# A new table of unit order and of engines for flexible units, in a cluster-attention and maxout-FFN kernel on one core

## The chip, the core and the metric

The kernel runs on one core of one Trainium2 chip. The metric is the device time in microseconds (us) of one execution. A measurement of this kernel can tell a difference of about 0.2% (1.4 us) from none.

## What is computed

Four batches of eight heads; each head has 768 queries and 768 keys of 64 numbers. A query sees only the keys whose nearest centroid (of 16 per head) is the query's own. The attention's output goes through a feed-forward network (FFN) with three first matrices, of whose products the largest is kept.

```python
q_assign = argmax(q_n . c_n);  k_assign = argmax(k_n . c_n)      # 16 clusters per head
mask     = q_assign[:, None] == k_assign[None, :]
scores   = where(mask, scale * q @ k.T, -1e9)
attn     = softmax(scores);  x = attn @ v                        # (4, 8, 768, 64) -> (3072, 512)
h        = max(x @ w1, x @ w2, x @ w3)                           # 512 -> 768
out      = h @ w_out                                             # 768 -> 512
```

The result is wanted nearly as exact as fp32, so most operands of a matmul are held as a high and a low f16 half, and a product is made of three matmuls.

## The kernel before

The program writes its work as 3077 **units**, each a closure that issues one instruction or one matmul group on one engine: TensorE (PE), VectorE (DVE), ScalarE (ACT), GpSimd (POOL), or a DMA on SyncE's queue (SP). No scheduler moves them at run time: each engine runs its instructions in the order in which they were written, and waits at an instruction whose inputs are not there or whose buffer is still in use.

- **prep** (lines 690 to 885), once for each of 4 batches and 4 pairs of heads: q and k are loaded, a power of two that scales them is found (L733 on DVE or L731 on ACT, then small instructions L739 to L762), both are cut into halves (L810/L812, L378/L382, L818), and the cluster of each row becomes 32 further rows of the operands (L577 to L648), so that the score matmul itself adds the mask.
- **v_prep** does the same for v. **weights** loads the four matrices in 24 pieces (`piece`, L1019 to L1030: a cast L1024 or L1026 on ACT or POOL, then one DVE instruction L1030), finds scales (L1070, for w_out L1094 to L1108) and cuts into halves (L1041/L1043, L987/L989, L1046).
- **visit**: 32 visits (batch, half of the queries, pair of heads), each of six tiles of 128 queries by 768 keys. A tile (`tile_units`) is a score product on PE into PSUM (L1256 and L1258, buffer `big`, of which there are three), the row minimum on DVE (L1267), the exponential on ACT (L1273), for later batches the row scale (L1293, L1294, L1321/L1323), and the two halves `hl` (L378, L380 or L382; L1279 or L1332). They are then transposed by a DMA (L1282); of the first 40 steps every second is transposed on PE instead (L1304) and split from PSUM (L378 or L382, then L1312). After six tiles comes the product with v on PE (`av`, L1207, 36 matmuls), and its result is split into `x16` (L380/L382 and L1179).
- **ffn**: eight groups of 384 tokens. A group has 18 first products (`hid`, L1413, 12 matmuls into the PSUM buffer `one`, of which there are two); each is evicted (`ev`: L380 on ACT or L382 on DVE for the first of three, L1427 on DVE for the others, which takes the maximum), each third eviction is cut into halves (L987/L989, L1142); then three output products (`outp`, L1468, 18 matmuls), evicted by L380 or L382 and stored.

The order around everything is a table: `ORDER` lists the 3077 unit numbers. `HANDS` gives a letter (V, S, G, Q for DVE, ACT, POOL, SP) for each of those units that may run on more than one engine. Two of the few lines that use them:

```python
u.hand = engines[next(hands)] if u.pick else None     # Plan.run: the engine of a flexible unit
u.fn(u.hand) if u.pick else u.fn()                    # Plan.run: issued in ORDER's order
```

A unit that needs a buffer takes the place that came free first, so the table also sets which place of `big`, `one` or `stage` is used by whom.

Of the kernel before, what the change touches and what calls it, by code (L numbers as in the profile page):

```python
# [1534 lines left out]
```

## Time and profile before

| what | us |
|---|---|
| median of three runs | 711.62 (711.52 to 713.02) |
| span of the profiled execution, first to last instruction | 709.1 |
| what lies around it (median less span) | 2.5 |
| PE busy in the span | 665.5 |
| DVE busy | 599.0 |
| ACT busy | 483.6 |
| POOL busy | 403.3 |

A row of the windows names a stretch and says how long each engine was busy in it. A row of the instruction groups gives line, engine, operation, what is written and read, the count, the summed busy time, the mean of one in ns, and the idle time of the engine just before, with what ended it. In a timeline row the first number is the start, the second the duration.

### The profile page before, as it was taken

What the parts mean: (1) busy time and instruction counts of PE and PEld (TensorE: products, weight loads), DVE (VectorE), ACT (ScalarE), POOL (GpSimd) and SP (SyncE); (2) the same over time, 40 slices, a digit from 0 to 9 for tenths busy, and PEclk for the clock granted to TensorE, in tenths of its full rate; (3) what the DMA queues carried; (4) which work ended last, traced back from release to release, by engine and by line L of the source; (5) the groups of instructions that cost most, each with busy time, mean ns of one, the idle gap of its engine ahead of it and who ended that gap; (6) DMA issues with size and microseconds to landing.
All of it is one profiled execution on the core that took longest, in us unless ns stands there. A gap on an engine that the chain in (4) does not pass through costs nothing. (4 is left out here: it accounts for less than half of the span.)

```text
span 709.1 us, 13176 instructions
## 1 busy us (share of the span) xinstructions
PE 665.5 (94%) x4505; PEld 389.9 (55%) x4505; DVE 599.0 (84%) x1470; ACT 483.6 (68%) x841; POOL 403.3 (57%) x374
## 2 busy tenths in 40 slices
PE   3778778998999999999999999999999999999997
PEld 1554545555456655565555555655555646564663
DVE  7998999999998878999989888999899967784231
ACT  6988989989865657787767647786667775651000
POOL 3677887888656564857566545666584551531000
PEclk8578999999999999999999999999999999999999
DMA  6698878779798879998979998999999785775001
GB/s 225 199 216 182 207 210 205 188 174 202 168 196 188 172 126 217 197 185 195 215 156 194 179 189 181 185 196 196 197 194 178 145 164 112 148 158 125 1 1 60
DMA packets 297795, 121.03 MB, mean 171 GB/s; under 512 B 273024, under 2 KB 284160, under 8 KB 297728
## 3 DMA queue, kind: packets, MB, share of 16 engines
q1 hardware_dynamic: 297728, 120.20, 80.0%
q8 instruction: 35, 0.57, 0.3%
q14 instruction: 32, 0.26, 0.1%
HBM read 31.49 MB, written 6.29 MB: 53 GB/s over the span
## 5 line engine op out<-in xcount | busy, mean ns | idle before, releaser
L1267 DVE TENSOR_SCALAR_CACHE_REDUCE big<-big,nsc 128x768 f32<-128x768 f32 x192 | 192.7, 1016 | 11.4 <-PE big L1258 10.8
L1413 PE MATMUL one<-x,w16a 128*128 128x384 f16 x1152 | 197.0, 326 | 0.2
L1279 POOL TENSOR_TENSOR hl<-e,hl 128x768 f16<-128x768 f32 x86 | 144.4, 1682 | 61.1 <-ACT hl L378 34.2
L1413 PEld LDWEIGHTS <-w16a 128*128 128x128 f16 x1152 | 111.5, 98 | 75.7 <-issue 2.9
L1273 ACT ACTIVATE e<-big,nm 128x768 f32<-128x768 f32 x116 | 104.4, 901 | 49.7 <-DVE big L1267 32.3
L1256 PE MATMUL big<-qk 128*128 128x512 f16 (+1 forms) x384 | 96.6, 334 | 12.2 <-ACT e L1273 9.4
L1207 PE MATMUL big<-pt,v 128*64 128x384 f16 x1152 | 101.8, 330 | 2.4 <-ACT e L1273 1.4
L1413 PE MATMUL one<-x,w16b 128*128 128x384 f16 x576 | 98.9, 326 | 1.0 <-DVE worow L1098 1.0
L1258 PE MATMUL big<-qk 96*128 96x512 f16 (+1 forms) x384 | 96.1, 331 | 0.1
L1273 ACT ACTIVATE big<-big,nm 128x768 f32<-128x768 f32 x76 | 66.3, 872 | 43.7 <-DVE big L1267 35.3
L1207 PEld LDWEIGHTS <-v 128*64 128x64 f16 x1152 | 70.0, 111 | 33.2 <-issue 9.8
L1413 PEld LDWEIGHTS <-w16b 128*128 128x128 f16 x576 | 55.7, 98 | 40.1 <-issue 3.4
L1332 DVE SCALAR_TENSOR_TENSOR hl<-big,rs,hl 128x768 f16<-128x768 f32 x72 | 72.7, 1011 | 4.6 <-ACT hl L380 3.6
L380 ACT ACTIVATE hl<-big,rs 128x768 f16<-128x768 f32 x62 | 55.7, 898 | 27.3 <-issue 10.7
L1323 POOL TENSOR_SCALAR e<-e,rs 128x768 f32<-128x768 f32 x37 | 34.0, 919 | 65.9 <-DVE rs L1294 47.1
L1256 PEld LDWEIGHTS <-qk 128*128 128x128 f16 x384 | 35.3, 99 | 43.7 <-issue 22.1
L378 ACT CAST hl<-e 128x768 f16<-128x768 f32 x60 | 49.8, 831 | 5.3 <-POOL e L1323 4.5
L1258 PEld LDWEIGHTS <-qk 96*128 96x128 f16 x384 | 38.2, 100 | 27.1 <-issue 2.6
L818 POOL TENSOR_TENSOR qk<-stage,qk 128x768 f16<-128x768 f32 x26 | 43.8, 1686 | 9.2 <-ACT qk L378 5.5
L1468 PE MATMUL one<-wo,vf_h 128*128 128x512 f16 x216 | 48.3, 379 | 0.5 <-ACT o L380 0.4
L1468 PE MATMUL one<-wo,wf_h 128*128 128x512 f16 x216 | 48.3, 379 | 0.0
L1427 DVE SCALAR_TENSOR_TENSOR wf_h<-one,wf_h 128x384 f32<-128x384 f32 x48 | 26.5, 553 | 20.2 <-PE one L1413 19.6
(203 smaller groups left out, 1002.0 us busy)
## 6 DMA issues: line engine op xcount, KB each, us to landing
stage<-in_qk_dram SPq DMA_DIRECT2D x32, 384.0 KB, 4.3
wd<-in_moe_w_dram SPq DMA_DIRECT2D x18, 512.0 KB, 4.2
out_dram<-o SPq DMA_DIRECT2D x24, 256.0 KB, 2.9
qk<-qk SPq DMA_DIRECT2D x15, 384.0 KB, 4.3
qk<-qk SPq DMA_DIRECT2D x30, 192.0 KB, 3.5
stage<-in_v_dram SPq DMA_DIRECT2D x12, 384.0 KB, 4.0
wd<-in_moe_w_out_dram SPq DMA_DIRECT2D x6, 512.0 KB, 3.8
qk<-cl_t SPq DMA_DIRECT2D x60, 48.0 KB, 2.3
```

Of the source, the lines that this page charges most:

```text
L378: eng.copy(out, x)
L380: eng.activation(out, x, AF.Copy, scale=k)
L818: eng.tensor_tensor(t()[:, AQ, i], x(), t()[:, BQ, i], op=ALU.subtract)
L1207: nc.tensor.matmul(t()[D * i : D * i + D, 0:nb], v()[:, i, kt, a], pts[i % len(pts)]()[:, rows[i], c * QT + kt, :], start=(m == 0), stop=( ...
L1256: nc.tensor.matmul(t()[:, lo:hi], aq[:, qs], ak[:, lo:hi], start=True, stop=False)
L1258: nc.tensor.matmul(t()[:, lo:hi], bq[0:K2, qs], bk[0:K2, lo:hi], start=False, stop=True)
L1267: nc.vector.tensor_scalar(s, s, -SCALE if exact else nscs[:, b, pr : pr + 1], 3.0e38, op0=ALU.mult, op1=ALU.min, accum_out=nm())
L1273: nc.scalar.activation(e(), t()[:, 0:S], AF.Exp, bias=nm(), scale=-1.0, accum_out=r)
L1279: eng.tensor_tensor(hl()[:, 1, :], e(), hl()[:, 0, :], op=ALU.subtract)
L1332: eng.scalar_tensor_tensor(hl()[:, 1, :], e(), r(), hl()[:, 0, :], op0=ALU.mult, op1=ALU.subtract)
L1413: nc.tensor.matmul(t()[:, 0:nb], w16[jt // JA][:, jt % JA, wa, i, ct], x16[b, gi, ct]()[:, xa, 0:nb], start=(m == 0), stop=(m == 3 * CT - 1),)
L1468: nc.tensor.matmul(t()[:, 0:DM], h16(jt)[:, ha, tt * P : (tt + 1) * P], wo16[0][:, jt, wa, :], start=(m == 0), stop=(m == 3 * JT - 1),)
```

## The change

`ORDER` and `HANDS` have new contents; no other line is touched. The table has five lines fewer, so a line number in the changed kernel is five smaller (L1267 becomes L1262). All units, their dependencies, the number of buffers and the sum of work on PE and on SP (475 and 372 units) stay. Units on DVE go from 1272 to 1265, on ACT from 619 to 608, on POOL from 339 to 357. The first and last lines of each table:

```diff
 ORDER = """
-1 0 18 19 51 52 173 445 151 2-5 7 6 54 53 8-15 20 21 30 22-24 39 25 26 40 27 55 28 16 31 33 36 35 56 41 57 63
+0 3 1 2 4 19 18 5-14 21 15 30 16 52 51 20 22 17 53-56 23 173 174 24 57 39 25 63 58 26 62 27 59 28 33 40 151 176
...
 HANDS = """
-VVSSSSSSVVSSSSSSGSGSGGQQGVSSGSGSVGQQGVSSSSGSSGQQGVSGGSVGSSGSSGGSGVSSGSSGSSGSSGVGSGSSGVSGSGGVVSGSGGSGGGGGVSGGSS
+VVSSSSSSVVSSVSVSGSGSGGQQGVSSGVGSGGQQGSSSSSGSSGQQGVSSGSGGSSGGSGGSSVSSGSSGSSGSSSVGSGSSGGSGSSSVSSGSGGSGGSGGVGSGSSGS
...
```

What the table moves is read from the order of the instructions on an engine. **First place: DVE, around the weight pieces of w_out, before the fifteenth first product of the first FFN group.** `wf` and `worow` belong to the pieces of w_out, `vf_h` to the FFN's evictions, `big` to the score tiles. Before:

```order
L626 STREAM_TRANSPOSE cl_t_1639<-onehot2_99 128x768
L1030 SCALAR_TENSOR_TENSOR wf_1838<-wd_1852,top_111 128x512
L1267 TENSOR_SCALAR big_1946,nm_1983<-big_1946,nsc_117 128x768
L1094 TENSOR_REDUCE worow_121<-wf_1838 128x1
L1142 TENSOR_TENSOR vf_h_1497<-vf_h_1311,vf_h_1497 128x384
L1102 TENSOR_SCALAR worow_121<-worow_121 128x1
L382 TENSOR_SCALAR vf_h_1311<-one_1951 128x384
L1098 TENSOR_SCALAR worow_121<-worow_121 128x1
```

The same place in the change:

```order
L1025 SCALAR_TENSOR_TENSOR wf_1835<-wd_1861,top_111 128x512
L1262 TENSOR_SCALAR big_1949,nm_1954<-big_1949,nsc_117 128x768
L1097 TENSOR_SCALAR worow_121<-worow_121 128x1
L1089 TENSOR_REDUCE worow_121<-wf_1835 128x1 x2
L1093 TENSOR_SCALAR worow_121<-worow_121 128x1
L1262 TENSOR_SCALAR big_1958,nm_1997<-big_1958,nsc_117 128x768
L1422 SCALAR_TENSOR_TENSOR vf_h_1320<-one_1965,vf_h_1320 128x384
L1097 TENSOR_SCALAR worow_121<-worow_121 128x1 x2
L1093 TENSOR_SCALAR worow_121<-worow_121 128x1
L621 STREAM_TRANSPOSE cl_t_1633<-onehot2_99 128x768
L1422 SCALAR_TENSOR_TENSOR vf_h_1320<-one_1979,vf_h_1320 128x384
```

The eviction L382 of the product before has left DVE, and the last conversion of a w_out piece, two row maxima and the transposition L626 stand later against the FFN's products.

**Second place: ACT, at the same point of the program.** Before:

```order
L1273 ACTIVATE e_1923,rs_1578<-big_1861,nm_1902 128x768
L987 CAST x16_1925<-xs_1826 128x384
L378 CAST hl_1927<-e_1923 128x768
L1041 ACTIVATE wf_1838<-wf_1838,w_s_1911 128x512
L987 CAST vf_h_1497<-vf_h_1311 128x384
L987 CAST wo16_1103<-wf_1838 128x512
L1273 ACTIVATE e_1991,rs_1824<-big_1946,nm_1983 128x768
```

In the change:

```order
L1036 ACTIVATE wf_1589<-wf_1589,w_s_1923 128x512
L982 CAST vf_h_1527<-vf_h_1320 128x384
L982 CAST x16_1942<-xs_1833 128x384
L1184 ACTIVATE rs_1570<-rs_1570 128x6
L375 ACTIVATE vf_h_1320<-one_1925 128x384
L1268 ACTIVATE e_1946,rs_1770<-big_1912,nm_1920 128x768
L726 ACTIVATE qk_1879,q_m2_1880<-stage_1900 128x768
```

The eviction (L375, before L382 on DVE) is now ACT's, between a row sum and an exponential.

**Third place: ACT at the start, from the first maxima of pair 1 to the first four mask rows.** Before:

```order
L731 ACTIVATE qk_170,q_m2_171<-stage_0_156 128x768
L731 ACTIVATE qk_170,q_m2_171<-stage_0_154 128x768
L488 ACTIVATE cw_100<-one_180 64x4x16 x4
L380 ACTIVATE qk_186<-stage_0_150,q_s_211 128x768
L380 ACTIVATE qk_186<-stage_0_152,q_s_211 128x768
L847 COPY qk_186<-qk_186 64x1536 x3
```

In the change:

```order
L483 ACTIVATE cw_100<-one_166 64x4x16 x4
L726 ACTIVATE qk_195,q_m2_196<-stage_0_184 128x768
L375 ACTIVATE qk_168<-stage_0_153,q_s_227 128x768
L375 ACTIVATE qk_168<-stage_0_155,q_s_227 128x768
L842 COPY qk_168<-qk_168 64x1536 x4
L373 CAST qk_195<-stage_0_186 128x768
```

One of the two maxima (L731) has gone to DVE, and the four copies stand together.

## Rows read from the trace of the kernel before

**Rows 1.** The page, first part: busy time, share of the span, instructions.

```profile
PE 665.5 (94%) x4505; PEld 389.9 (55%) x4505; DVE 599.0 (84%) x1470; ACT 483.6 (68%) x841; POOL 403.3 (57%) x374
```

**Rows 2.** Windows: stretch, its length, busy time (and count) by engine, clock, DMA.

```profile
0.00:115.70 115.70, 82.67 (x554) 53.43 (x555) 105.39 (x227) 99.30 (x177) 82.58 (x99) 0.87 0.80 204
115.70:160.28 44.58, 42.16 (x306) 25.66 (x307) 44.28 (x107) 41.10 (x76) 36.22 (x32) 1.00 0.77 194
160.28:211.90 51.62, 48.86 (x332) 27.50 (x331) 50.53 (x135) 41.73 (x71) 34.03 (x32) 1.00 0.91 189
211.90:640.00 428.10, 426.60 (x2920) 247.78 (x2919) 377.88 (x965) 294.65 (x509) 247.66 (x208) 1.00 0.90 177
640.00:709.10 69.10, 65.20 (x399) 35.55 (x397) 20.95 (x39) 6.84 (x12) 2.76 (x4) 1.00 0.18 46
```

**Rows 3.** PE's waits from 115.7 to 211.9: total us, times, longest.

```profile
PE one L1413 <- DVE worow L1098: 1.0, 1, 1.0
PE one L412 <- DVE vf_h L1427: 0.7, 1, 0.7
```

**Rows 4.** PE's timeline at the fifteenth first product of FFN group one.

```profile
160.28 2.11 PE L1413 MATMUL one<-x,w16b 128*128 128x384 f16 x12 [0.96 <-DVE worow L1098]
```

**Rows 5.** DVE's timeline just ahead of that product.

```profile
156.28 1.42 DVE L1030 SCALAR_TENSOR_TENSOR wf<-wd,top 128x512 int32<-128x512 int32 x1
...
158.55 0.68 DVE L1094 TENSOR_REDUCE worow<-wf 128x1 f32<-128x512 f32 x1
...
159.68 0.54 DVE L382 TENSOR_SCALAR vf_h<-one 128x384 f32<-128x384 f32 x1
```

**Rows 6.** Instruction groups of DVE by form, whole span.

```profile
L626 DVE STREAM_TRANSPOSE cl_t<-onehot 128x768 f16<-128x768 f16 x14 | 13.6, 972 | 0.2
...
L1279 DVE TENSOR_TENSOR hl<-e,hl 128x768 f16<-128x768 f32 x10 | 10.6, 1057 | 0.3
...
L382 DVE TENSOR_SCALAR hl<-e 128x768 f16<-128x768 f32 x13 | 7.2, 552 | 0.6 <-ACT e L1321 0.6
...
L733 DVE TENSOR_REDUCE q_m<-stage 128x1 f32<-128x768 f32 x7 | 6.5, 945 | 0.3 <-DMA stage<-in_qk_dram 0.3
...
L1043 DVE TENSOR_SCALAR wf<-wf,sc_s 128x512 f32<-128x512 f32 x2 | 1.5, 740 | 0.0
```

**Rows 7.** Instruction groups of ACT by form, whole span.

```profile
L380 ACT ACTIVATE vf_h<-one 128x384 f32<-128x384 f32 x18 | 8.7, 486 | 0.7 <-PE one L1413 0.7
L1024 ACT CAST top<-wd 128x512 f16<-128x512 bf16 x11 | 8.6, 778 | 1.1 <-DVE wf L1030 0.8 <-DMA wd<-in_moe_w_dram 0.3
```

**Rows 8.** ACT's waits from 115.7 to 160.28.

```profile
ACT e L1273 <- DVE big L1267: 2.8, 4, 1.0
```

**Rows 9.** DVE's timeline at the two waits for PE between 53 and 59 us.

```profile
53.96 1.02 DVE L1267 TENSOR_SCALAR_CACHE_REDUCE big<-big,nsc 128x768 f32<-128x768 f32 x1 [0.99 <-PE big L1258]
...
58.66 0.56 DVE L1226 TENSOR_TENSOR xs<-big,xs 128x384 f32<-128x384 f32 x1 [1.28 <-PE big L1207]
```

**Rows 10.** Line L1030 (min/median/max in ns), and one slow instance beside POOL's timeline.

```profile
L1030 DVE SCALAR_TENSOR_TENSOR wf<-wd,top x24: 672/692/1945, 19.8 to 156.3; 128x512 int32<-128x512 int32 x24
...
43.47 1.95 DVE L1030 SCALAR_TENSOR_TENSOR wf<-wd,top 128x512 int32<-128x512 int32 x1
...
43.22 1.64 POOL L1279 TENSOR_TENSOR hl<-e,hl 128x768 f16<-128x768 f32 x1
```

**Rows 11.** SP's queue and ACT's timeline: a load of batch 1, its reader; DMA landings.

```profile
3.55 0.51 SPq L725 DMA_DIRECT2D stage<-in_qk_dram  x1
...
112.33 4.22 SPq L1282 DMA_TRANSPOSE pt<-hl  x2
...
127.23 0.89 ACT L731 ACTIVATE qk<-stage 128x768 f16<-128x768 f32 x1
...
stage<-in_qk_dram SPq DMA_DIRECT2D x32, 384.0 KB, 4.3
```

**Rows 12.** The timeline's last instruction on an engine.

```profile
705.23 0.69 ACT L380 ACTIVATE o<-one,so 128x512 f32<-128x512 f32 x1 [3.20 <-PE one L1468]
```

More of the change, by code (lines that the diff above doesn't have):

```diff
@@ L155 @@
[L155 to L157 removed]
+0 3 1 2 4 19 18 5-14 21 15 30 16 52 51 20 22 17 53-56 23 173 174 24 57 39 25 63 58 26 62 27 59 28 33 40 151 176
[29 rows of a table added]
+1252 432 1281 1248 434 525 433 370 371 2636 1273 1274 1287 357 385 386 358 1282 1283 359 1284 387-390 378 1288
[9 rows of a table added]
@@ new lines @@
+551 1360 547 1390 1366 521 522 1377 1361 2669 1387 511 523 1378 2670 1367 481 482 548 1391-1393 1379 2673 1397
[4 rows of a table added]
+1438 1443 1444 1429 566 1453 1445 1430 569 1454 1416 568 1425 1439 1446 1455 1456 1447-1449 2691 1406 1431 583
+2653 2688 1440 2692 1432 1407 1463 2693 1464 1441 1442 1408 1471 1472 577 1465 1466 2694 2695 1473 2701 1488
+1489 1450 1433 2697 1457 1458 578 579 2696 629 1459 1474 1490 1475-1478 1505 2698 1491 1492 1467-1469 1480 1506
+2699 2700 2702 2703 1481 1460 1507 1508 2704 1509 1510 1493 1461 1497 1482-1484 1470 1485 1479 1494 1462 1486
@@ new lines @@
+2708 1525 1517 1495 1496 1511 1498 1499 1512 1500 1501 1526 1502 1527 2709 1528 1503 1513 1504 1487 2710 2714
+2715 584 1518 1534 1535 1519-1521 1542 1536 1543 1522 1537 1523 2711 1544 1538 1539 1529 1540 1545 1551 1552 628
+1530-1532 1514 1515 1553 1554 1516 1571 1546 1572 1559 1560 1555 2712 1547 1524 1573 2717 2718 1561 1556 2719
+1548 1557 1562 2766 1549 1579 1574 1563 1588 2720 1575 585 586 1533 1580 1581 2721 1589 1590 1558 1550 1541
+1564-1567 587-592 1591 1582 593 598 1596 2722 1583 1592 1597 1576 1577 2725 2727 595 599 1593 1598 1599 1594
[3 rows of a table added]
@@ new lines @@
+1604 1578 639 1644 1645 636 1630 602 674 1619-1621 604 1646 1651 2737 1636 1637 1631 1647 1652 2741 637
+1638-1640 1667 1659 2738 638 640 1653 1648 1668 1654 610 1641 2739 2740 643 644 611 1669 612 1670 1655 1660 645
+1649 613 2743 1679 1622 676 1656 675 2742 1680 677 1671 1661 1662 678 616 2745 1623 1672 641 708 615 1632 1657
+614 617 2767 2744 1624 679 680 1663 1681 1687 681-683 2746 1664 1682 1683 1673 1665 2749 2751 1704 1688 1684
+1685 1705 2747 1689 2750 688 642 2748 1674 1696 1666 685 686 689 1697 2752 648 718 646 1706 1698 650 1690 2753
@@ new lines @@
+1658 651 687 1713 2754 1699 1700 1675 1714 652 1707 1691 709 1701 1715-1718 2755 1708 653 649 647 1702 654-656
[5 rows of a table added]
+1748 626 1778-1780 627 1795 1731 1732 667 1812 1813 668 1787 1788 2777 719 721 1814 1804 701 669 1757 1781 722
[5 rows of a table added]
+2798 1846 1832 739 2799 729 1833 1852 1853 1847 2800 1866 812 1860 1861 1834-1836 744 2801 1854 1867 745 2802
[4 rows of a table added]
+1931 1908-1911 1932-1934 1922 2820 1937 2945 2822 1935 2823 2824 1949 1923-1925 1936 1919 1893 1950 1938 1926
+1927 1939 1940 1894 1941 1942 1902 2828 1943-1945 2946 1951-1954 1957 2831 1958-1960 1955 1966 1967 2829 1974
@@ new lines @@
+1975 762 1968 2830 1983 1961 1976 1928 1969 1984 1970 1971 1962 1985 1963 1986 1977 1987 1978 2834 2832 2835
+1988 1989 1946 1972 1947 1948 1991 2003 2011 2837 1992 1964 1990 2839 1993 769 768 1994 2012 1973 2004 2838
+1979-1981 1965 1956 2013 1995-1998 770 771 2005 2028 2840 2029 811 2836 1999 2006 2014 2007 772 2020 773 2008
+774 2015-2017 2021 2841 2842 2009 2022 2030 2018 2886 2845 2846 2023 2843 2844 775 2887 2031 2024 776 2025 2032
+2033 2847 1982 2019 2010 2045 2037 2046 2026 2849 781 2038 778 782 2047 2065 2000 783 2048 2034 2049-2051 2039
@@ new lines @@
+2848 2850 2851 777 2035 2066 2040 2067 814 2041-2043 2853 2852 813 779 2068 2069 780 2833 2027 2057 2058 2854
[4 rows of a table added]
+2867 796 2081 797 787 2089 801 800 799 871 868 2870 825 798 2868 2119 2873 2128 2120 2113 2105 2114-2117 2129
[4 rows of a table added]
+2158-2160 876 2161 2177 2892 2170 903 804 2183 2888 2171 878 2184 2889 879 2190 2191 2185 880 2186 881 805 2192
+2187 904 2199 2200 806 882 905 867 2193 883 2890 2152 2201 2894 2178 807 2202 884 808-810 2203 2194 2204 2179
+906 2188 2162 2205 2163 2164 2180 907 2207 2219 2172 2195 2895 2196 2227 2897 2208 2209 2228 2236 2197 908 2220
@@ new lines @@
+909-911 885 877 891 2189 2899 892 2237 875 2898 2229 2221 2206 2222 2210 2223 2900 2238 916 913-915 2239 886
+2240 936 2198 2901 2902 2211 2230 888 2903 917 2904 918 2241 2212 2905 2253 937 2224 2906 2213 2231 2242 2225
+2254 846 890 2907 2244 2908 2255 2245 847 2181 887 889 2909 2214 2215 2243 2232-2235 2896 2913 2273 2246 848 849
[5 rows of a table added]
+2893 898 2303-2305 2313 2218 855 2931 2933 2327 2318 2319 2335 2270 2328 2336 2329-2332 2932 2337 943 2320 899
+2321 900 2338-2340 2333 2322 2271 944 2344 2934 2345 2306 2272 2937 2352 2346 2353 2354 2941 2347 2348 2938 2355
@@ new lines @@
+2341 2342 2935 2369 2361 2334 2323 2349 2939 2370 2356 2350 3065 2936 2362 2371 2389 2357-2359 2372 2940 2390
+2391 2363 2314 2324 2381 2942-2944 2948 2360 2343 2364 2365 2351 2382 2325 2366 2392 2367 2368 2326 2373 2383
+2393 2394 2374 2406 2398 2951 2949 2384 2375 2376 2385 2407 2386 2408 2950 2395 2399 945 2387 2415 2409
+2400-2403 2396 2388 2377 2423 2416 2417 2424 2425 2418 2404 2410 2411 2419 2420 2954 2443 2378 2412 2413 2405
+2426 2444 2955 2427 2421 2397 2445 2379 2952 2380 2435 2452 2469 2453 2454 2428 2455-2457 2957 2470 2436
@@ new lines @@
+2429-2431 2446 2447 2958 2458 2471 2437 2959 2961 2460 2960 2461 2962 2965 2462 2448 2414 2422 2472 2473
+2438-2440 2966 2963 2964 2441 2463-2465 2449 2969 2474 2450 2967 2477 2478 2432 2479 2968 2970 2475 2442 2466
+2433 2497 2476 2489 2467 2468 2459 2451 2956 2973 2498 2499 2480 2506 2481 2974 2971 2490 2491 2434 2482 2507
+2975 2492-2494 2508 2972 2976 2483 2514 2509 2500 2510 2501 2515 2981 2511 2512 2977 2484 2495 2978 2523 2531
+2485 2502 2516 2517 2496 2983 2486 2518 2519 2979 2520 2521 2532 2503 2504 2524 2982 2525 2533 2526 2980
@@ new lines @@
+2527-2529 2984 2543 2985 2551 2544 2534 2487 2535 2986 2545 2536 2522 2513 2488 2552-2555 2991 2989 2990 2530
+2953 2537 2538 3006 2987 2546 2547 2988 2992 2560 2568 2569 2993 2997 2556 2548 2549 2557 2570 2571 2558 2994
+2561 2995 2539 2998 2550 2505 2559 2585 2577 2586 2572 2573 2562 2587 2578 2999 3001 2579 2996 3000 2540 3002
+2588-2590 3003 3004 3011 2563 2564 2580 2581 3007 2574 2565 3012 2541 2591 2582 2575 2576 2566 2583 2584 2567
+3008 3014 2592 2593 3009 2542 3010 3013 3015 2594-2596 3017-3019 3021 3020 3022 3025 3023 3026 3027 3024
@@ L158 @@
+3028-3031 3033 3034 3032 3035 3037 3036 3066 3038 3041 3042 3039 3043 3045 3040 3044 3046 3049-3051 3053 3047
+3048 3052 3054 3057-3059 3061 3055 3056 3060 3062-3064 3068 3067 3069 3016 3071-3073 3070 3074-3076
 """
 HANDS = """
-VVSSSSSSVVSSSSSSGSGSGGQQGVSSGSGSVGQQGVSSSSGSSGQQGVSGGSVGSSGSSGGSGVSSGSSGSSGSSGVGSGSSGVSGSGGVVSGSGGSGGGGGVSGGSS
-GSSVSGSVSSGSSGSSGSGSVSSGGGGSSGGSSGSSSGSSGGSSGGGSSGGGSGSVSGGSSGQQGGVGSVSSSSGGGGQQGGVGSGSSVGGSSVQQGGVGSGSSGVGSSG
-QQVGVSGGSVGSGGSGQQVGVSGGVSSSGSVGQQGGVSSGVSGGGSSGQQGVVSSGSSSVGGGVQQGGVSSGSSGSGGSVQQVGVGSGSVSSGVSGQQVGVSSVSSGSGG
@@ L169 @@
-VSGSVVSGSVVVGVVVGGVVVVVSVSSVVVGSVVSGSVVSGSVVSGSVVVGSVVSGSSSVVVGGVVVSGVVVSGSVVSGSVVGGVVVGVSSVVVVSGSVVGGSVVGGVVV
-VGSVVSGSVVVVVSSVVVGGSVVGGSVVVGSVVGVSVVVVVVVGGSSSSVVSVSVVVVVVVSGSVVVVVVVVGSVVGVVVVVVVSVVVVSGVVVSVVVVGVSVVVVSVVV
-VVSS
+VVSSSSSSVVSSVSVSGSGSGGQQGVSSGVGSGGQQGSSSSSGSSGQQGVSSGSGGSSGGSGGSSVSSGSSGSSGSSSVGSGSSGGSGSSSVSSGSGGSGGSGGVGSGSSGS
+SVSGSVGGGSSGSSGSGSVSSGSSGGGGGGSGSSSGSSGGSSSGGSSGSGGGSVSGGSSGQQGGVSSGSSSGGSSGQQVGVSGGSSSVVSGGQQGGVGVGSSGSGGGGQQGG
+VSGGSSGGGVSGQQGGVSGGSSSGGGGGQQGGVGSGSSSGGGGGQQGGVGGGVSSGGGSVQQGVVVGGVSSGGSSGQQGGVGGGSSSGGSSGQQVGVSSVVSGGGSGGQQVV
@@ new lines @@
+VSGGVSGGGGVGQQGGVSSGSVGSSGSSGSGGSGGSSGVSGVSGSGGSSGSSGVGVSSGSSGSSGSSVSSGSSGSSGSSGSSGSSVSSGSSGSSGSSGSVSGSSGSVSGVVG
+GSVSGSVGSVGVGSVSSGVVSGGSSVSGGSVSSGSVSSGSSVSSGSVVGGVVSGGVSVGGGSVGSGSVGSVVSVGSGSVSVGVVGGGSSVSSGSVVGGVVSGGSSVGVGSVS
+GGSVSSGSSVSSGSVSVGSVGGGVSVSSGVVGSGSVGGVSSVGSGSVSSGSVSSGSSVSSGSVGSGSVSGGVSVSGGVVSGGSVGVGVSVSVGVVGGGVVGGGSSVGGVVVG
+GVVVGSGSSVGGGVVGSGSVGSGSVVGGGSVGSGSVSSGVSVGSGSVSSGSVSGGVSVGVGSVGSGSVSGGSSVSGGSVGGGSVGGGSVVGGGSVGGGSVSVGVSVSGVSVS
+GGVVSGGSVVSVVSVGSGSVSVGVSVSVGSVVSGSVGGGSSVGSGVVSSGVVVGVVSVVVGSVVSGSVVSGSVVSGSVVSGSVVVVSSSSVVVGSVVSVSVVGGSVVGGSVV
@@ L172 @@
+SGSVVVVVSSSVVGGSVVGGSVVGGSVVSGSVVSGSVVSVSSVSVVSGSVVSGSVVVGSVVSVVVVVGSVVGVSSSSVVSGSVVSGSVVSGSVVVGSVVGGSVVSGSVSSVV
+VGSVVSGVVVSVSVVGGSVVSGVVVVVVSVSVVGGSVVGVSVVSGSVVGGSVVVGVVVSVSSVVVVSVSVVSVVVVVVVVVVVSVVVGSVVVVSVS
 """
```

22 lines of the change are left out of this document (removed), and 184 rows, old and new, of the table ORDER.

## Prediction

> **What bounds the kernel now.** I read the page first: PE is busy 94% of the span, DVE 84%, ACT 68% [rows 1]. The change leaves PE's work as it is, so it can only give or take PE's idle time: 709.1 - 665.5 = 43.6 us. The windows say where that lies [rows 2]: 115.70 - 82.67 = 33.03 us before 115.70, then 2.42, then 2.76, then only 1.50 in the 428 us to 640.00, and 3.90 in the last stretch. These 3.90 are the eviction of the last output, which starts at 705.23 [rows 12], and its store. So up to 211.9 PE waits, and from there on it sets the pace alone.
>
> Who is late before 211.9? DVE is busy 44.28 of 44.58 us and 50.53 of 51.62 us in the second and third stretch, 98.5% of both together, ACT 92% and 81%, POOL 81% and 66% [rows 2]. PE's waits name DVE for the longest two [rows 3]. The longest stands before the fifteenth first product of the first FFN group, at 160.28 [rows 4]. DVE's timeline shows why: the eviction that frees the PSUM buffer for this product, L382 at 159.68, stands behind a conversion of a w_out piece (L1030, 1.42 us), a score tile and a row maximum of w_out (L1094, 0.68 us) [rows 5], and w_out is wanted only by the output products, 18 us later in the program. The reader is to see two things in these rows: DVE is a queue without slack, and not everything in it is urgent.
>
> **The change, part by part.** I count, for a product on PE that has the same PE work ahead of it in both orders, the DVE instructions that must run ahead of it. Durations are those of the rows.
>
> *Up to the product at 115.70* (third first product of FFN group one). DVE's work ahead stays at about 105 us: twelve instructions leave it or are put off, eight come, 0.3 us less in all. ACT gets 2.8 us more, mostly five casts L1024 that were POOL's (0.778 each [rows 7]), less what it gives away; it has 115.70 - 99.30 = 16.4 us idle there [rows 2]. POOL's work ahead stays within 0.4 us. I take 0 for this part. Bounds: at the very start a maximum over q goes from ACT to DVE (0.945 [rows 6]) and stands ahead of the scales of pair 0, and the first score tile's minimum gets 1.4 us more DVE work ahead of it, so up to +1.4; by the tile at 42 us the sum is even again. In the other direction, DVE idles 0.99 and 1.28 us for PE between 53 and 59 us [rows 9], and an order that fills both gaps is worth up to -2.3.
>
> *Up to the product at 160.28.* By a change of hand DVE loses twelve instructions: five of the form hl<-e (0.552), two of L1043 (0.740), two evictions (0.54 [rows 5]), one L1279 (1.057) and two more small ones of about 0.55, together 7.5 us. It gains eight: one maximum L733 (0.945), a split from PSUM (at most an L1279, 1.057) and six of 0.3 to 0.55, together about 5 us [rows 6]. Put off to behind the product are one L1030 (1.42), two L1094 (0.68 each [rows 5]), the transposition L626 (0.972 [rows 6]) and eleven small ones for the scales, about 0.1 us each: 4.8 us. That is 7.3 us of durations. A DVE instruction starts some 0.08 us before the one ahead ends (in rows 5, 158.55 + 0.68 is past the next start), and 15 fewer of them make it 6 us. Against a PE idle of 2.42 us in this stretch DVE is then no longer the late one. ACT is next: it gets six casts L1024 (4.7 us) and the two evictions (0.486 each [rows 7]) ahead of this product, gives others away, and has 0.7 us more within the stretch: 41.10 + 0.7 = 41.8 us against PE's 42.16 [rows 2]. An engine in order cannot be that full without making PE wait. What speaks for it is that 2.8 of ACT's 3.5 idle us here are waits for the score minimum on DVE [rows 8], which comes earlier now. I take half of the idle time, -1.2; bounds 0 and -2.4.
>
> *Up to the product that starts at 211.90.* DVE's work ahead is 8.5 us less than before, so another 2.5 in this stretch, by the same kinds (one L1279 and two splits to POOL, two score minima of later tiles put off). ACT's is 0.5 us less than before, so here it is relieved by 4. Nothing else is near full. I take -2.5 of the 2.76; bounds -0.5 (a fifth) and -2.76.
>
> *From 211.9 to 640.* What was put off comes back here: DVE 377.88 + 6 us, POOL 247.66 + 21 us (instructions from ACT and DVE), ACT 13 us less, against 426.60 us of PE [rows 2]. PE waits only 1.5 us now, so there is nothing to gain. I take 0; bounds -0.5 and +3. The three us would be the worst of a few places where a product now stands closer behind its eviction. The last stretch has the same output products in another order and the same end: 0.
>
> *SP.* No DMA is added. The seventh issue, a load for batch 1 at 3.55 us, moves to behind a transposition of pair 1, and its partner to behind the transpositions at 112.33; the readers on ACT run from 127.23, and a load lands in 4.3 us [rows 11]. The cover is some 8 us, and the transpositions of visits are not later in SP's queue than they were. 0.
>
> Sum: 0 - 1.2 - 2.5 + 0 = -3.7 us, from a span of 709.1 to 705.4. The median is 2.5 us above the span of the profiled execution, so **711.6 - 3.7 = 707.9 us**.
>
> **DVE and POOL side by side.** One L1030 took 1.95 us where the median is 0.692, at 43.47; POOL's subtraction L1279 ran from 43.22 to 44.86, and DVE ended 0.56 us after it [rows 10]. So a DVE instruction can stand still for up to 1.25 us beside POOL. The Trainium skill (SBUF — State Buffer, "Practical consequences") says that a DVE instruction with two inputs in SBUF and a GpSimd instruction that reads SBUF exclude each other for their whole length; the row agrees. It speaks against this change, which gives POOL 18 more units. By the rows: 18 times 1.25 is 22 us of DVE at most, and nearly all of these come after 211.9, where DVE has 428.10 - 377.88 - 6 = 44 us to spare [rows 2]. POOL's work ahead of the product at 211.90 is the same within 0.4 us. I add nothing to the sum; the case in which it decides is the third rival.
>
> **The rivals.**
>
> 1. *More is gained early.* The order fills the gaps of rows 9 and PE gets all of 2.42 and 2.76: -5.2 - 2.3 = -7.5, 704.1 us. For it: 33 of the 43.6 idle us lie there. Against: DVE's work ahead is the same at 115.70, and DVE is 91% busy there already.
> 2. *No change.* ACT takes DVE's place: it is as full as PE in the second stretch, and each late exponential holds a PSUM buffer of three. Only 2.5 us or less would be left, and with the +1.4 of the start the result is within 0.2%: 711.6 - 2.5 + 1.4 = 710.5 us. It also covers a table whose new DVE order is no relief, because DVE's total falls by 2 us only and the rest is put off: at the output products DVE has 4.2 us less ahead, not 8.5.
> 3. *Slower.* After 211.9, DVE instructions stand behind POOL's longer list, and the PE product behind them waits. The room between an eviction and its product is a few tenths at the closest places, so a hit of 1.25 us costs about 0.95. Four hits eat the 3.7; six make 5.7 and the time 711.6 - 3.7 + 5.7 = 713.6 us. It decides when PE's idle time from 211.9 to 640 grows from 1.5 to over 5 us. Against it: DVE is 88% busy there, and PE's idle time is 0.4% of the stretch at present [rows 2].
>
> **How the numbers follow.** A difference under 0.2%, 1.4 us, can't be told from none. Forecast (705.5 to 710.2): 0.57. Rival 1 (below 705.5): 0.13. Rival 2 (710.2 to 713.0): 0.16. Rival 3 (over 713.0): 0.14. So faster 0.70, same 0.16, slower 0.14. The range leaves out rival 3 (0.14) and the far end of rival 1 (0.06): 704.0 to 713.0 us. The forecast's own range is the 705.5 to 710.2 above.
>
> **What would show it.** Right: PE's idle time from 115.7 to about 207 falls from 5.2 to 1.5 us, the wait before the fifteenth first product is gone, DVE's share there falls to some 94%, ACT's rises to 95% before 157 us, and PE's idle time before the product of 115.70 stays within 2 us of 33. Wrong: that product comes 2 us earlier or later, so that the start decides; PE's waits in the second stretch name ACT; or idle time of PE appears after 211.9.

## The result, and the profile after

The changed kernel takes **719.93 us** (median of 7 runs, 715.30 to 722.08), before 711.69 us (7 runs, 710.32 to 714.24). The ratio over all these runs is 1.0095, with a 95% interval of 1.0070 to 1.0121: 6.8 us slower (the medians alone are 8.2 us apart), where 3.7 us faster was forecast and 713.0 us was the end of the range. The profiled execution of the change took 720.24 us, with a span of 718.5 us, 9.4 more than the 709.1 of before. The rows of after follow in the order in which those of before stand above; line numbers are five smaller.

The page, first part [rows 1]:

```profile
PE 668.4 (93%) x4505; PEld 390.8 (54%) x4505; DVE 599.2 (83%) x1463; ACT 470.0 (65%) x829; POOL 420.5 (59%) x392
```

No engine has more to do, apart from POOL's 17 us; PE's 2.9 us more are the same 4505 matmuls, some of which take longer. PE's idle time went from 43.6 to 50.1 us. The windows say where [rows 2]. The first three borders are the starts of the same products as before (115.70, 160.28 and 211.90 us there). The border at 640.00 lies inside a product; the same matmul starts at 648.55 us in the change, 0.25 us ahead of the border in these rows:

```profile
0.00:117.94 117.94, 84.39 (x555) 54.12 (x555) 104.65 (x225) 101.39 (x178) 80.77 (x97) 0.86 0.79 199
117.94:160.22 42.28, 41.91 (x307) 25.48 (x306) 41.47 (x97) 40.71 (x76) 33.68 (x30) 1.00 0.88 201
160.22:209.85 49.63, 48.00 (x333) 26.86 (x331) 46.08 (x131) 39.04 (x70) 34.78 (x31) 1.00 0.90 182
209.85:648.80 438.95, 428.98 (x2922) 248.03 (x2919) 383.96 (x969) 280.71 (x494) 267.62 (x232) 1.00 0.90 174
648.80:718.50 69.70, 65.09 (x398) 36.34 (x396) 23.01 (x46) 8.11 (x16) 3.63 (x3) 1.00 0.19 50
```

- First stretch: 117.94 against 115.70 us, 2.24 lost. PE's idle time is 33.55 us against 33.03; the rest is 1.7 us more of busy time for the same work.
- Second and third: 42.28 + 49.63 = 91.91 against 44.58 + 51.62 = 96.20 us, **4.29 gained** (forecast 3.7).
- Fourth, up to the same matmul: 438.95 - 0.25 = 438.70 against 428.10, **10.60 lost**. PE idles 9.97 us there; it was 1.50. The other 2.1 us are longer busy time of the same matmuls.
- Last: 69.70 + 0.25 = 69.95 against 69.10, 0.85 lost (forecast 0).

In the second and third stretch DVE is now busy 87.55 of 91.91 us, 95.3%, where it was 98.5%. PE's waits there no longer name the row maxima of w_out [rows 3]. From 117.94 to 209.85 all of them are:

```profile
PE big L1251 <- ACT e L1268: 1.6, 2, 1.2
PE big L1251 <- DVE hl L1274: 0.3, 1, 0.3
```

The fourth stretch has sixteen waits of PE. From 209.85 to 648.8:

```profile
PE big L1202 <- DMA pt<-hl: 2.8, 4, 1.8
PE big L1251 <- DVE hl L1327: 1.7, 4, 0.8
PE big L1251 <- ACT e L1268: 1.4, 2, 0.8
PE big L1251 <- DVE rs L1288: 0.9, 1, 0.9
PE big L1251 <- DVE x L1174: 0.6, 1, 0.6
PE one L407 <- DVE wf_h L1422: 0.6, 1, 0.6
PE one L744 <- DVE q_m L738: 0.6, 1, 0.6
PE one L1408 <- DVE rs L1288: 0.5, 1, 0.5
PE big L1251 <- DVE cl_t L572: 0.3, 1, 0.3
```

Together they are 9.4 us. Before, from 211.9 to 640, there were three rows, four waits and 1.1 us in all:

```profile
PE big L1207 <- ACT e L1273: 0.5, 2, 0.3
PE big L1256 <- DVE hl L1332: 0.3, 1, 0.3
PE big L1256 <- DVE x L1179: 0.3, 1, 0.3
```

The reader is to see the new first row: four products with v stand still for a transposition (`pt<-hl`, SP's queue), which never happened after 212 us before. PE's timeline shows the longest:

```profile
252.91 0.35 PE L1202 MATMUL big<-pt,v 128*64 128x384 f16 x1
255.01 3.08 PE L1202 MATMUL big<-pt,v 128*64 128x384 f16 x35 [1.75 <-DMA pt<-hl]
```

One matmul starts at 252.91, the other 35 only at 255.01; the product takes 5.2 us instead of 3.1. All four such products (252.91, 374.01, 493.15 and 513.45 us) together take some 4.1 us longer, of which 2.8 are the idle time in the row. SP's timeline ahead of it:

```profile
235.78 1.17 SPq L641 DMA_DIRECT2D qk<-cl_t  x2
...
241.04 0.90 SPq L720 DMA_DIRECT2D stage<-in_qk_dram  x1
241.99 0.43 SPq L1477 DMA_DIRECT2D out_dram<-o  x1
243.53 5.96 SPq L1277 DMA_TRANSPOSE pt<-hl  x3
249.55 0.57 SPq L720 DMA_DIRECT2D stage<-in_qk_dram  x1
250.21 6.21 SPq L1277 DMA_TRANSPOSE pt<-hl  x3
```

The last transposition that this product needs issues at 250.21, though its half tile was written by 246.03: it stands behind three other transpositions (5.96 us for three, the first two of them under way or done by then) and a load whose reader is far off. Before, the same issue went out at 246.66, 0.2 us after its input, as the third of these five:

```profile
242.80 13.18 SPq L1282 DMA_TRANSPOSE pt<-hl  x5
```

A second case: for the product that waits at 493.15 us in the change, one issue goes out 11.2 us after its input is ready (478.87 to 490.05); before it was 0.03 us.

These are not two odd cases. For each of the 137 transpositions that issue behind the product of 211.90 in both kernels I took the time from the end of the instruction that writes its half tile to its issue: 2.17 us on average before, 3.23 in the change. For the 35 ahead of it the averages are 2.90 and 3.74.

Rows of the list that name DVE can lead to SP as well. The timelines of ACT and DVE ahead of PE's waits at 324.46 (`hl`, 0.78 us) and 487.85 (`rs`, 0.88 us):

```profile
322.45 0.90 ACT L375 ACTIVATE hl<-big,rs 128x768 f16<-128x768 f32 x1 [1.98 <-DMA pt<-hl]
...
486.82 0.98 DVE L572 STREAM_TRANSPOSE cl_t<-big 128x768 f32<-128x768 f32 x1 [0.75 <-DMA qk<-cl_t]
```

Both had their inputs. They waited for a place that a DMA was still to read: one of the four `hl` tiles, and the only `cl_t`. So the reader should follow a named engine one step further back before he blames it.

### The profile page after: what moved, and what is told of

The parts are those of the page before. It is cut to its first block, busy times and chain, and to the rows that moved or that the text cites. A ratio compares the mean times of both kernels' runs of the same rounds, so it can differ in the third digit from the quotient of the medians.

```text
span 718.5 us, 13165 instructions
## 1 busy us (share of the span) xinstructions
PE 668.4 (93%) x4505; PEld 390.8 (54%) x4505; DVE 599.2 (83%) x1463; ACT 470.0 (65%) x829; POOL 420.5 (59%) x392
## 5 line engine op out<-in xcount | busy, mean ns | idle before, releaser
L1262 DVE TENSOR_SCALAR_CACHE_REDUCE big<-big,nsc 128x768 f32<-128x768 f32 x192 | 193.4, 1017 | 16.6 <-PE big L1253 15.9
L1274 POOL TENSOR_TENSOR hl<-e,hl 128x768 f16<-128x768 f32 x88 | 146.8, 1670 | 69.4 <-ACT hl L373 35.4
L1251 PE MATMUL big<-qk 128*128 128x512 f16 (+1 forms) x384 | 97.2, 335 | 21.5 <-ACT e L1268 14.3
L1202 PEld LDWEIGHTS <-v 128*64 128x64 f16 x1152 | 68.4, 110 | 35.5 <-issue 13.3
L375 ACT ACTIVATE hl<-big,rs 128x768 f16<-128x768 f32 x55 | 49.2, 898 | 30.1 <-DVE rs L1289 8.3
L1251 PEld LDWEIGHTS <-qk 128*128 128x128 f16 x384 | 34.8, 100 | 55.5 <-issue 28.2
L377 POOL TENSOR_SCALAR hl<-e 128x768 f16<-128x768 f32 x35 | 29.4, 841 | 36.7 <-ACT e L1316 19.1
L1318 POOL TENSOR_SCALAR e<-e,rs 128x768 f32<-128x768 f32 x33 | 30.2, 916 | 31.9 <-DVE rs L1289 29.2
L813 POOL TENSOR_TENSOR qk<-stage,qk 128x768 f16<-128x768 f32 x28 | 46.0, 1645 | 4.6 <-ACT qk L373 3.9
L1137 POOL TENSOR_TENSOR wf_h<-wf_h 128x384 f16<-128x384 f32 x13 | 12.9, 989 | 57.0 <-DVE wf_h L984 50.0
```

Source lines behind the costliest of these rows:

```text
L375: eng.activation(out, x, AF.Copy, scale=k)
L813: eng.tensor_tensor(t()[:, AQ, i], x(), t()[:, BQ, i], op=ALU.subtract)
L1202: nc.tensor.matmul(t()[D * i : D * i + D, 0:nb], v()[:, i, kt, a], pts[i % len(pts)]()[:, rows[i], c * QT + kt, :], start=(m == 0), stop=( ...
L1251: nc.tensor.matmul(t()[:, lo:hi], aq[:, qs], ak[:, lo:hi], start=True, stop=False)
L1262: nc.vector.tensor_scalar(s, s, -SCALE if exact else nscs[:, b, pr : pr + 1], 3.0e38, op0=ALU.mult, op1=ALU.min, accum_out=nm())
L1274: eng.tensor_tensor(hl()[:, 1, :], e(), hl()[:, 0, :], op=ALU.subtract)
```

## Experiments

In all diffs `A` is the change's table, `B` that of before, and a number the position in the order; a unit keeps the engine that its part's table gives it. Each kernel ran 4 to 12 times, with before beside it; the text ahead of each result was written before it ran. Since one execution can differ by some us from the next in the first 100 us, stretches are compared by the start of products that have the same PE work ahead of them in every order. This table is worked out from the PE timelines: each product's start less its start in before (us).

| kernel (one profiled execution each) | 115.70 | 211.90 | 231.27 | 290.05 | 412.83 | 655.22 |
|---|---|---|---|---|---|---|
| the change | +2.23 | -2.05 | -0.13 | +2.00 | +4.30 | +8.89 |
| first part alone | +0.92 | -4.78 | -0.96 | -0.81 | -0.70 | -0.45 |
| last part alone | -0.85 | -1.02 | -1.01 | -0.79 | +1.42 | +5.04 |
| middle part alone | -0.27 | -3.93 | +0.15 | +0.30 | +0.26 | +0.27 |
| middle part, chain early | -1.32 | -3.11 | -1.47 | +1.05 | +1.22 | +2.73 |
| SP by readers | +0.78 | -3.91 | +1.71 | +1.47 | +8.17 | +11.88 |
| SP by readers and places | +0.32 | -5.44 | -3.88 | -3.64 | -0.35 | +0.54 |
| two joints | -3.07 | -7.06 | -5.21 | -4.74 | -3.45 | -1.68 |

### Which part of the table costs

```diff
 first part alone:  ORDER = A[0:1085] + the other units as in B
 last part alone:   ORDER = B[0:1085] + the other units as in A
 middle part alone: ORDER = B[0:460] + those of A[0:1085] that are left, as in A + the other units as in B
```

> The first 1085 units in the change's order and with its engines (up to about 210 us), all later units in the order and with the engines of before. Theory A (the loss lies in the order after 212 us; what came before gained): the first product after this point came 2.05 us earlier in the trace of the change, and the order of before adds nothing after it, so 711.7 - 2.0 = 709.7 us, ratio 0.997. Theory B (what was put off early comes due late, whatever the later order): PE's idle time from 212 to 640 stays near the change's 10 us instead of 1.5, and the time is 716 us or more.

Measured: 712.78 us, ratio 1.0011 (0.9983 to 1.0040).

> The reverse: the first 1085 units as before, the later ones in the change's order and with its engines. Theory A: PE idles 10 us instead of 1.5 from 212 to 640 and the time is 711.7 + 9 to 11 = 721 to 723 us, ratio about 1.014. Theory B: the later order alone costs little, 711 to 714 us.

Measured: 717.80 us, ratio 1.0085 (1.0054 to 1.0116).

> Only the stretch between units 460 and 1085 (about 100 to 210 us) from the change, the start and all after it from before. Theory A with the clock (the change lost 2.2 us between 84 and 100 us, where the granted clock fell to 0.50, and gained 4.3 us between 100 and 212): 711.7 - 4.3 = 707.4 us, ratio 0.994. Rival (the gain of the middle is only the start's loss made up, since PE came late and found its inputs ready): no more than 2 us of gain, 709.7 us or above.

Measured: 711.29 us, ratio 0.9989 (0.9964 to 1.0014).

The last part alone carries the loss: +0.85% there and +0.11% for the first part make +0.96%, and the change has +0.95%. In its size theory A was off: 6.0 us, not 9 to 11. And neither run with the gain of the middle is faster than before: 711.29 us is what the rival in the third text forecast (709.7 or above). Its mechanism, that the gain only makes up a late start, does not fit: in that run the product of 115.70 comes 0.27 us early, and the stretch from there to 211.90 still gains 3.66. Of all runs of this document, the ten traces with the change's order in this stretch gain 1.8 to 6.0 us in it; the four with the order of before lie between 0.2 us of gain and 1.6 of loss. So the gain is real, and it is lost behind 211.90. The table shows why: the product of 211.90 comes 4.78 and 3.93 us early, that of 231.27 only 0.96 us early or not at all. Theory B is not right either, since the waits do not go on: with the first part alone PE waits 4.3 us behind that product, 3.2 of them in the first 25 us, and from 231.27 to the end the lead shrinks by 0.5 only. In the run with the middle part alone PE, DVE, POOL and SP show the chain:

```profile
203.86 1.64 POOL L895 TENSOR_TENSOR v<-stage,v 128x768 f16<-128x768 f32 x1
...
205.56 0.53 SPq L940 DMA_DIRECT2D stage<-in_v_dram  x1
...
213.53 0.93 DVE L943 TENSOR_REDUCE vmax<-stage 128x1 f32<-128x768 f32 x1
...
223.11 0.62 DVE L1170 SCALAR_TENSOR_TENSOR x<-big,cv,x 128x384 f16<-128x384 f32 x1
...
223.78 0.49 PE L1247 MATMUL big<-qk 128*128 128x512 f16 x2 [2.41 <-DVE x L1170]
```

The change moves a split of v (L895) from DVE, where it ran at 183.34 us in before, to POOL (203.86 us here, 205.74 in the change). Its end frees the `stage` place for the next v tile, so that load issues at 205.56; in before SP has it 13 us earlier:

```profile
192.13 0.37 SPq L949 DMA_DIRECT2D stage<-in_v_dram  x1
```

Its maximum on DVE, its scales and the scaling of x follow, and the `big` buffer of the score product at 223.78 is free only after that.

### Mending that chain

```diff
 POOL
 L895 TENSOR_TENSOR v_2320<-stage,v_2320 128x12x64
-L571 TENSOR_TENSOR cl_t<-cl_t 128x24x16
-L1270 TENSOR_TENSOR hl<-e,hl 128x768
-L373 TENSOR_SCALAR hl<-e 128x768
-L580 TENSOR_TENSOR cl_t<-cl_t,cl_m 128x24x16
-L1270 TENSOR_TENSOR hl<-e,hl 128x768
 L895 TENSOR_TENSOR v_2442<-stage,v_2442 128x12x64
+L571 TENSOR_TENSOR cl_t<-cl_t 128x24x16
...
```

The five rows follow behind. With it the load (L940) stands behind the load before it on SP, the maximum (L943) behind the maximum before it on DVE, the scales and the scaling of x (L968, L373, L1170) ahead of the next row minimum, the product of the scales (L403) ahead of two others on PE, and one eviction on ACT ahead of a split and a scaling.

> The run with the middle part alone (711.3 us), with one chain mended: the second half of a v tile's split on POOL (L931) moved from 203.86 to 195.3 us, into a gap, so that the load of the next v tile issues at about 197 instead of 205.6 us, its maximum on DVE (L943) follows at 205 instead of 213.5, and the five small scale instructions behind it stand ahead of a score tile's minimum. Theory CHAIN (the 4.3 us gained before 212 us are given back because this load was put off, and the PSUM buffer of the score product at 223.78 us stays held until x is scaled): that wait, 2.41 us, goes, 709 us, and the lag to before at 230 us is -2 us or more. Theory AMOUNT (DVE simply has as much work ahead again by 225 us, whichever stands first): the wait moves to another product, within 0.7 us of 711.3.

Measured: 711.58 us, ratio 1.0006 (0.9986 to 1.0027). (The line L931 in that text is L895 in the kernel.) The wait at that product falls from 2.41 to 0.35 us, and others come: 1.41 us at a first product at 206.18, whose eviction now stands behind the earlier maximum, 1.40 us at 233.31 and 0.66 at 243.15. So the wait moved, as AMOUNT has it. But this run still joins two orders at unit 1085, which leaves a third reading: the loss is made where the two are joined.

### The joint

```diff
 two joints:   ORDER = B[0:460] + those of C[0:1366] that are left, as in C + the other units as in B
 later joint:  the same with C[0:1554]
               (C: the change with SP by readers and places, below)
```

> A version that could beat both: units up to 460 (about 100 us) as before, 460 to 1366 (to about 285 us) in the change's order and on its engines with SP's queue by readers and places, all after it as before. In the last run but two the lead over before was 3.8 to 4.8 us at 200 us and still 3.5 us at 270 us. Theory JOINT (the 3.8 us that the run with the middle part gave back at 212 to 229 us came half from joining two orders in the middle of a chain; 1.7 us come from the change's own order): a lead of 2 us or more stays to the end, 709 to 710 us. Theory LOAN (the lead is DVE work put off, and falls due wherever the order of before takes over): within 1 us of before.

Measured: **709.78 us, ratio 0.9978 (0.9959 to 0.9996)**: 1.6 us faster than before, the only version here that beats both.

> The same with the second joint at unit 1554, about 310 us. Theory JOINT: as the run with the joint at 285 us, 709 to 710 us, or a little slower, since the lead in the trace with SP's queue re-sorted was 2.9 us there. Theory LOAN: before's time or above.

Measured: 713.18 us, ratio 1.0018 (0.9992 to 1.0045).

For the joint at 285 us the time lies between the two theories: the 1.6 us have an interval of 0.3 to 2.9, so LOAN's "within 1 us of before" is not excluded by it. The trace speaks for JOINT only in part: the lead is 7.06 us at the product of 211.90, still 4.74 at 290.05 and 3.45 at 412.83, in the order of before by then, but 1.68 at 655.22. Of the 7.06, 3.07 were there at 115.70 by the luck of the start. So the middle of the change gains some 4 us, of which the runs' time keeps 1.6. By these single traces about half of what the first two hybrids gave back was the price of a joint in the middle of a chain: between the products of 211.90 and 231.27 they lost 3.82 and 4.08 us, this run 1.85, and the change itself, without any joint, 1.92. The later joint has the time of before, as LOAN has it, but it falls into another such place: a product with v takes 7.1 us, from 324.87 to 331.95. It waits 1.98 us for a transposition, and then its 35 matmuls take 4.74 us, which took 3.08 in the change at 255.01: the granted clock is 0.52 (near half, 1.2 GHz) from 327 to 330 us:

```profile
327.21 4.74 PE L1202 MATMUL big<-pt,v 128*64 128x384 f16 x35 [1.98 <-DMA pt<-hl]
```

### Order, engines, and one stretch of the last part

```diff
 engines only:  ORDER = B;                  HANDS of A for the units behind B[0:1085]
 order only:    ORDER of last part alone;   HANDS = B
 one stretch:   ORDER = B, but units A[2124:2424] (444 to 515 us) as in A
```

> The order of before throughout; only the engines of the flexible units after unit 1085 are the change's. Theory ENGINES (the loss after 212 us comes from the work given to POOL and from ACT to DVE, whose results arrive later): 712.1 + 4 to 6 = 716 to 718 us, with PE waiting for DVE's L1323 and for ACT after 212 us. Theory ORDER (the places in the queues cost, not the engines): within 1.4 us of before, 710.7 to 713.5 us.

Measured: 763.32 us, ratio 1.0726 (1.0701 to 1.0751).

> The first 1085 units as before, the later ones in the change's order, but all flexible units on the engines of before. Theory ORDER: as the run with order and engines, 717.8 us. Theory ENGINES: 714 us or less.

Measured: 765.00 us, ratio 1.0755 (1.0729 to 1.0781).

> Before, with 300 units (2124 to 2424 of the order, about 444 to 515 us) in the change's order and on its engines; it is the stretch in which the run with the whole later part lost 2.9 us. Theory LOCAL (each loss is made where it is seen, by a product placed behind an instruction that ends too late): 712.1 + 2.9 = 715 us. Theory CARRIED (the loss builds up from work put off earlier): not over 713 us.

Measured: 719.38 us, ratio 1.0101 (1.0073 to 1.0129).

None of these theories stands. Order and engines cannot be told apart: either alone costs over 50 us, so each order holds only with the engines that it was made for. With the engines alone, PE waits most for DVE's second halves:

```profile
PE big L1247 <- DVE hl L1323: 10.8, 12, 2.2
PE big L1247 <- ACT e L1264: 7.4, 10, 1.4
```

The one stretch costs 7.2 us, more than the whole last part (6.0 us) that contains it. Its first wait, 2.00 us at 456.48 us for an exponential, is not in the change, and behind it the granted clock falls to 0.50 (458 to 460 us), which it does not do in the change's fourth stretch (1.00): a joint again. It says nothing on where the change loses.

### SP's queue

The first kernel sorts the 246 issues of SP after unit 1085 by their readers alone; all other engines keep the change's order.

```diff
-SP's units behind A[0:1085]: as in A
+SP's units behind A[0:1085]: whichever has its input, the one first whose reader started first (less the transfer)
```

> The change, with nothing altered but the order of the DMA issues on SP after unit 1085: each stands by the time at which its reader ran in the trace of the change, less the transfer, so that transpositions no longer stand behind loads and mask rows wanted later. Theory SP (late transpositions): the four waits of PE for a transposition that the change has and before has not, 1.75 + 2.07 us at the product at 252.91 us and 0.80, 1.34 and 0.98 us at those of 374.01, 493.15 and 513.45 us, some 6.5 us in all, go: 719.9 - 6 = 714 us, ratio to before about 1.003. Theory POOL/DVE (DVE and ACT instructions that stand behind POOL's longer list): no more than 1 us goes, 719 us, and PE's waits after 212 us name DVE and ACT as before.

Measured: 723.59 us, ratio 1.0170 (1.0133 to 1.0206), slower still, so neither theory's time came. (Theory SP's 6.5 us also count each of the four waits twice, once alone and once inside its product; from the four products there were 4.1 us to win.) The four waits for transpositions are gone; one came elsewhere. The largest new loss is on DVE:

```profile
344.39 0.98 DVE L564 STREAM_TRANSPOSE cl_t<-big 128x768 f32<-128x768 f32 x1 [4.23 <-DMA qk<-cl_t]
```

The mask rows (`qk<-cl_t`) had been put off, since their reader is far; but the tile `cl_t` that they read has one place, and DVE's next transposition must wait for it. A score product behind it cost PE 2.40 us, the next one 1.26, and then the granted clock was 0.50 from 348 to 352 us. A DMA has two customers: who reads what it brings, and who next writes what it reads. The next kernel counts both. Of its new order on SP against the change's, the piece around 240 us:

```diff
-L720 DMA stage<-in_qk_dram 128x768
-L1477 DMA out_dram<-o 128x512
-L1277 DMA_TRANSPOSE pt<-hl 128x12x128 x3
-L720 DMA stage<-in_qk_dram 128x768
-L1277 DMA_TRANSPOSE pt<-hl 128x12x128 x7
+L1477 DMA out_dram<-o 128x512
+L1277 DMA_TRANSPOSE pt<-hl 128x12x128 x8
+L720 DMA stage<-in_qk_dram 128x768
+L1277 DMA_TRANSPOSE pt<-hl 128x12x128 x2
...
```

> The change, with SP's queue after unit 1085 in another order once more: each issue now stands by what waits for it of both kinds, the reader of what it brings and the next writer of the place that it reads (the transposed mask tile, of which there is one place, and the split score tiles, of which there are four); the first re-sorting left the second kind out and made DVE's transposition L563 wait 4.3 us at 340 us. 107 of 246 issues move. Theory SP (in the change most of the later waits of PE come from SP's queue: four products with probabilities for a transposition, 6.9 us with the waits inside them, three for a place that a transposition or a mask row still reads, 1.9 us, and two for a mask transposition, 1.2 us): 6 to 9 us go, 711 to 714 us. Theory QUEUES (the later order has too little room on DVE, ACT and POOL, and whatever is mended on SP is lost to the next engine): 718 us or more.

Measured: **715.60 us, ratio 1.0039 (1.0016 to 1.0062)**. Against the change's 1.0095 that is 0.56%, 4.0 us (1.5 to 6.5), from SP's order alone. The run with five neighbours changed (below), which keeps SP's order and ran beside this one, took 719.61 us, 4.0 more, too. (What that text calls L563 and 4.3 us is the row above, L564 and 4.23 us.) The time lies between the two theories, short of SP's 711 to 714 and clear below the 718 of QUEUES: SP's order is a cause, at two thirds of the least size that theory SP gave it (6 to 9 us, in which the four waits are again counted twice). The rest, 2.8 us, stays. The average time from a written half tile to its issue, over the 137 transpositions of above, is 2.21 us here, as in before (2.17; the change 3.23). The trace is the fastest of its 12 executions, so only its later part is compared: from the product of 231.27 to that of 655.22 the change loses 9.02 us, this kernel 4.42. PE's waits from 212 to the end are:

```profile
PE big L1251 <- ACT e L1268: 2.1, 3, 1.3
PE big L1202 <- ACT e L1268: 1.0, 2, 0.9
PE big L1251 <- DVE hl L1327: 0.8, 3, 0.3
PE big L1251 <- DVE x L1174: 0.6, 1, 0.6
PE one L407 <- DVE wf_h L1422: 0.6, 1, 0.6
PE big L1251 <- DVE cl_t L572: 0.6, 1, 0.6
```

Not only the row of `pt<-hl` is gone. So are the waits for `rs`, and of those for `hl` half, without a change of order on DVE, ACT or POOL. Those for exponentials have grown, from 1.4 to 3.1 us.

### Five neighbours changed

```diff
 DVE
-L1262 TENSOR_SCALAR big,nm<-big,nsc 128x768
-L1288 TENSOR_SCALAR rs<-rs 128x1
-L1289 RECIPROCAL rs<-rs 128x1
-L1327 SCALAR_TENSOR_TENSOR hl<-big,rs,hl 128x768
+L1327 SCALAR_TENSOR_TENSOR hl<-big,rs,hl 128x768
+L1262 TENSOR_SCALAR big,nm<-big,nsc 128x768
+L1288 TENSOR_SCALAR rs<-rs 128x1
+L1289 RECIPROCAL rs<-rs 128x1
...
 ACT
-L956 ACTIVATE stage<-stage,sc_s 128x768
-L1268 ACTIVATE e,rs<-big,nm 128x768
+L1268 ACTIVATE e,rs<-big,nm 128x768
+L956 ACTIVATE stage<-stage,sc_s 128x768
```

> The change with SP's queue as it is, and five instructions moved past their neighbours where PE waits 0.28 to 0.56 us for them: three splits and a cut on DVE (308, 450, 473 and 564 us) and an exponential on ACT (358 us). Theory LOCAL: the five waits go, 0.28 + 0.29 + 0.56 + 0.54 + 0.56 = 2.2 us, 719.9 - 2.2 = 717.7 us. Theory CARRIED (what is moved back makes the next product late): within 0.7 us of 719.9.

Measured: 719.61 us, ratio 1.0103 (1.0069 to 1.0137).

> The same with five instructions moved besides, as in the next run. Theory SP: 2 us below the run with SP alone, 709 to 712 us. Theory QUEUES: 717 us or more.

Measured: 716.04 us, ratio 1.0052 (1.0027 to 1.0077).

Neither gains. The first fits theory CARRIED: its ratio is that of the change, and from the product of 231.27 to that of 655.22 its trace loses 9.21 us, the change's 9.02; LOCAL's 2.2 us of gain would lie just outside the interval. The second is as the run with SP alone. My reading, which no run tests by itself, is that DVE is 87% busy in the change's fourth stretch, so that what one instruction gains there another pays.

## Why the prediction was wrong

- **The middle, -1.2 and -2.5.** Right in place and in cause: 2.30 and 1.99 us, 4.29 together, the first twice what was forecast. PE's idle time from 115.7 on fell from 5.2 to 2.0 us (forecast 1.5). Of the DVE work that I counted away ahead of 211.90, 8.5 us, the windows show 8.0 (from 200.20 to 192.20 us busy). (The "15 fewer" instructions are 19 by the prediction's own count, 4 by change of hand and 15 put off; that makes 5.8 us instead of 6.) DVE was the late one; with the row maxima of w_out put off, its share fell to 95.3% (forecast 94%) and ACT's rose to 40.71 of 42.28 us, 96% (forecast 95%). The run with two joints shows that a part of the gain, 1.6 us (0.3 to 2.9), can be kept.
- **The start, 0.** It cost 2.2 us in the change's profile, 0.8 past the bound of +1.4. PE's idle time is the same within 0.5 us. What is longer are matmuls, since the granted clock fell (next section), and it did not do so in every execution of that start. Over the six traces that begin with the change's order the product of 115.70 comes 1.54 us earlier to 2.23 later than in before's profile, 0.7 later on average; over the nine that begin with the order of before, 3.07 earlier to 1.09 later, 0.7 earlier on average. So the start may cost about 1.4 us, the bound; with this spread that is not shown.
- **"The transpositions of visits are not later in SP's queue than they were. 0."** This is the step that failed. The text gives a row only for the loads of the start; for the transpositions it gives none. They are later, behind 211.90 by 1.06 us on average (3.23 against 2.17 us from the written half tile to the issue), and 4.0 us (1.5 to 6.5) of the 6.8 go when only SP's order is mended.
- **"From 211.9 to 640: I take 0; bounds -0.5 and +3."** The bound failed with it. The work per engine came as counted (DVE 383.96 us, forecast 383.88; POOL 267.62, forecast 268.66; ACT 280.71, forecast 281.65), and "a few places where a product now stands closer behind its eviction" were to be the worst. Sixteen waits in nine rows came, 9.4 us, where there were four, 1.1 us, and the stretch lost 10.60 us. With SP's order mended its one trace still loses 4.96 us there (433.06 against 428.10), so the +3 looks too small without SP's share too; the 2.8 us that remain in the time are net of what was gained ahead of the stretch.
- **The rivals.** The third came true by its own test (PE's idle time from 1.5 to 10.0 us, "over 5") and on its side, at 719.9 instead of 713.6, but not in the main by its mechanism. It had DVE stand still beside POOL. For the 794 instructions after 212 us that run on DVE in both kernels, the durations summed over each trace differ by 2.6 us only, and PE's longest new row names a DMA. How much of these 2.6 us reaches PE is not shown. The prediction's own sign of being wrong, idle time of PE after 211.9, came; so did another, the product of 115.70 2.2 us later, though the start did not decide. The prediction's rivals all argue from work per engine; a queue whose work keeps its amount and changes its order, SP, was in none of them.
- **What stays open.** The 2.8 us that remain after SP's order was mended, and with them the 4.96 us that its trace loses behind 211.90: the waits there name mostly exponentials and halves of tiles, and single moves did not remove them. Which of the 216 units after 212 us that changed engine, or which moved rows, cost this was not settled, since order and engines could not be separated.

## What to carry to other kernels

A table that changes no work still changes when each buffer place comes free; price a moved step by asking for every DMA both who reads its target and who waits to overwrite its source, on every queue and over the whole program. When PE has 0.4% idle time in a long stretch, an order can lose there at hundreds of products and can gain next to nothing, so its bound is one-sided, and here it had to be wider than "a few places". Hybrids of two orders measure the joint as well as the parts: put the joint where few units differ and no chain is open, and try two positions before believing one.
